# Token tiles turned by DMA transposes instead of TensorE's, in an attention and two-expert-layer kernel

## The chip, the cores and the metric

The kernel runs on one core of a Trainium2 chip. The metric is the device time of one execution in microseconds (us); lower is better. The profile comes from one execution. In it PE is TensorE (PEld its weight loads), DVE is VectorE, ACT is ScalarE, POOL is GpSimd and SP is SyncE, whose queue issues all of this kernel's DMAs.

## What is computed

Inputs are 4 sequences of 576 tokens with 8 heads of 64. An attention with a memory term gives 512 numbers per token; two gated expert layers of 512 to 1536 to 512 follow.

```python
scores = scale * q @ k.T                      # causal
local = softmax(scores) @ v
q_p = where(q > 0, q, exp(q) - 1) + 1
mem_out = (q_p @ M_prev) / (q_p @ z_prev + 1e-6)
x = g * mem_out + (1 - g) * local             # g = sigmoid(beta); 2304 x 512
xn = x / sqrt(mean(x * x) + 1e-6) * rms_g     # first layer's norm
y = (silu(xn @ w_gate) * (xn @ w_val)) @ w_out
out = (sigmoid(y @ w_gate2) * (y @ w_val2)) @ w_out2
```

## The kernel before, in words

The 2304 tokens go in five groups. Group -1 holds the first 128 tokens of each sequence (512 tokens); its attention is written out by hand at the start. Groups 0 to 3 hold the other 448 tokens of one sequence each. The main loop (from line 976) takes a group through both expert layers, l = 0 and 1, each in NF = 12 slices of 128 hidden units: `hidden` makes the two products `pg` and `pv` of a slice (12 matmuls each, in `mm3`, line 782), `out_share` (line 831) adds the slice's 12 matmuls to the four output tiles `po`. While group g is in these layers, the attention of group g + 1 is done in 36 steps, listed by `att_steps` (line 905) and handed out at a fixed rate as the slices go by, all of them four slices ahead of the end (six in group -1). The last five steps are the norm (`att_norm`) and four times `next_xT`, one for each 128-token tile.

Matmuls contract over partitions, so the expert layers need a group's tokens with the 512 channels on partitions. The attention leaves them with tokens on partitions, in the tile `x`. `att_xT` (line 602) turns them: VectorE writes the normalized tile `xn` (line 605), TensorE transposes its four 128x128 blocks in float32 into a PSUM tile `pxt` (line 610), ScalarE copies that as float16 into the high half of the token tile `ha` (line 614), and VectorE writes the rest, PSUM minus high half, as float16 into the low half (line 615). A product then is three float16 matmuls per block of channels: high by high, high by low, low by high. The fourth tile overlaps the third by 64 tokens; only its last 64 are kept. `half_tokens` (line 900) makes the token tile of shape 128 x 2 x 4 x 512.

Tile pools: `ap_` (line 76) has one buffer for each name unless the call says otherwise; `xn` has two; `psa`, the PSUM pool of `pxt` and of the attention's products, has two. A new tile in a buffer waits until all that use the old one are through. The tile `x` has one buffer: the next sequence's values are loaded into it by `att_v` (lines 137 and 138) when the last `xn` has been written.

Weights come from device memory. Group -1 makes float32 and group 0 float16 parts of them once and stores these; later loads (lines 753 and 756) go into 13 slots in turn, on SP's queue, some slices ahead of their use. The same queue holds the loads of q and k (line 182), the stores of outputs (lines 889 and 894) and of weight parts (line 688).

The order of the instructions on each engine is not that of the text: the framework's planner goes through the program with durations that it assumes, and puts on each engine the ready instruction that comes first in the text. The hardware then runs each engine's list in that order.

Of the kernel before, what the change touches and what calls it, by code (L numbers as in the profile page):

```python
# [9 lines left out]
F32 = mybir.dt.float32  # L10
F32R = mybir.dt.float32r
F16 = mybir.dt.float16
# [4 lines left out]
ALU = mybir.AluOpType  # L17
# [39 lines left out]
def attn_moe_moe_kernel(ctx, tc, qT, kT, qk0, v, mz, beta, w8, rms_g, outT):  # L57
# [6 lines left out]
    nc = tc.nc  # L64
    B, H, D, S = qT.shape
    NP = H // 2
    DM = H * D
    KD = DM // 128
# [7 lines left out]
    ap_ = ctx.enter_context(tc.tile_pool(name="ap", bufs=1))  # L76
# [7 lines left out]
    ident = const.tile([128, 128], F32, name="ident")  # L84
# [4 lines left out]
        out=tri, in_=tri, compare_op=ALU.is_ge, fill=NEG, base=0, pattern=[[1, 128]], channel_multiplier=-1  # L89
# [35 lines left out]
    for i in range(2):  # L125
        t = const.tile([128, S], F32R, name=f"q2_{i}")
# [6 lines left out]
    st = {}  # L133
# [468 lines left out]
    def att_xT(g, t, xt):  # L602
        s = st[g]
        xn = ap_.tile([128, DM], F32, tag="xn", bufs=2, name="xn")
        nc.vector.scalar_tensor_tensor(
            out=xn, in0=s["x"][:, t, :], scalar=s["ri"][:, t:t + 1], in1=g_bc, op0=ALU.mult, op1=ALU.mult
        )
        ps = late["ps"].tile([128, KD, 128], F32, tag="pa", name="pxt")
        for k in range(KD):
            nc.tensor.transpose(ps[:, k, :], xn[:, k * 128:(k + 1) * 128], ident)  # L610
        o = 64 if t == 3 else 0
        c0 = 128 * t
        n = 128 - o
        nc.scalar.copy(out=xt[0][:, :, c0:c0 + n], in_=ps[:, :, o:128])
        nc.vector.tensor_tensor(
            out=xt[1][:, :, c0:c0 + n], in0=ps[:, :, o:128], in1=xt[0][:, :, c0:c0 + n], op=ALU.subtract
        )


    late, first_raw = {}, []  # L620
    ring = {"w": 0, "top": 0, "raw": 0}
# [76 lines left out]
    for i in range(2):  # L698
        t = const.tile([128, 512], I32, name=f"top{i}")
# [196 lines left out]
    def wide_tokens(tags):  # L896

        return [xp.tile([128, KD, NMAX], F32R, tag=t, name="x" + t) for t in tags]

    def half_tokens(tag):  # L900

        t = xp.tile([128, 2, KD, NMAX], F16, tag=tag, name="h" + tag)
        return [t[:, 0], t[:, 1]]

    def att_steps(g):
        yield lambda: att_v(g)

        for h in range(H + 1):
            if h < H:
                yield lambda h=h: att_qk(g, h)  # L910
                yield lambda h=h: att_scores(g, h)

            if h == 0:
                yield lambda: att_vmax(g)
            if h == 1:
                yield lambda: att_vsplit(g)
            if h > 0:
                yield lambda h=h: att_av(g, h - 1)
                if h % 2 == 0:
                    yield lambda h=h: att_mem(g, h // 2 - 1)  # L920
        yield lambda: att_norm(g, 0, 4)
        for t in range(4):
            yield lambda t=t: next_xT(g, t)

    def att_first():


        att_load0()
        xt = wide_tokens("ab")
        ws, hs = [[], []], [htiles(-1, 0, f) for f in range(2)]  # L930
        do = first_stages(xt)
        do.update(slice_stages(xt, ws, hs))
        traced, before = nc.cur_bb.bb.instructions, {}
        for name in ORDER.split():
            n = len(traced)
            if name.startswith("fill"):
                do["fill"](int(name[4:]))
            else:
                do[name]()
            for i in traced[n:]:  # L940
                if i.engine in before:
                    tc.add_manual_dep(
                        i,
                        before[i.engine].name,
                        mybir.DependencyInfo(mybir.DependencyClass.NoSync, mybir.DependencyReason.DATA),
                        reason="order",
                    )
                before[i.engine] = i
            if name == "Cb3":
                z["hi"] = before[mybir.EngineType.Activation]  # L950
            if name == "Vb3":
                z["lo"] = before[mybir.EngineType.DVE]

        ring["raw"] = 0
        return xt, ws, hs

    def next_xT(g, t):
        if t == 0:
            st["xt"] = half_tokens("a")
        att_xT(g, t, st["xt"])  # L960

    xt, early_ws, early_hs = att_first()
    zctx.close()
# [11 lines left out]
    for g in range(-1, B):  # L975
        n = 512 if g < 0 else S - 128
# [6 lines left out]
        for l in range(2):  # L983
# [5 lines left out]
            for f in range(NF + 1):  # L989
                if f < NF:  # L990
                    if f >= early:
                        if g > 0 and l == 1 and f == NWIDE:
                            mid = NF if g < B - 1 else NF // 2 + 2
                            for e, c in ((nc.vector, slice(NWIDE, mid)), (nc.gpsimd, slice(mid, NF))):
                                if c.start < c.stop:
                                    e.tensor_scalar(
                                        out=unit[2][:, c],
                                        in0=unit[1][:, c],
# [25 lines left out]
            xn = wide_tokens("cd") if l == 0 else None  # L1024
            for d in range(KD):
                evacuate(l, d, n, g, po[d], xn)
            if l == 0 and g >= 0:
                xh = half_tokens("b")
                halve_tokens(n, po, xh)
            if l == 0 and g < 0:  # L1030
                token_scale()
            xt = xn
        xt = st.pop("xt", None)
# [55 lines left out]
```

## Time and profile before

| | |
|---|---|
| median of 3 runs | 1075.39 us (1075.17 to 1077.75) |
| the profiled execution | 1077.86 us, with a span of 1076.1 us |
| TensorE busy | 97% of the span |
| VectorE, ScalarE busy | 69%, 51% |
| mean granted TensorE clock | 0.991 of full speed |
| DMA, mean | 203 GB/s |

Busy time is the time in which an engine runs an instruction; for TensorE the ends of pipelined matmuls are modelled, so overlapping matmuls of 0.35 us each may follow each other every 0.19 us. The chain of waits is followed back from the last instruction, at each step to what released it. "Issue to landing" of a DMA runs from its issue on SP to the moment when its completion is seen.

### The profile page before, as it was taken

Reading aid. Unit: us, or ns where it says so; the run is one execution under the profiler, and the core shown is the slowest. Engines: PE = TensorE matmul, PEld = TensorE weight load, DVE = VectorE, ACT = ScalarE, POOL = GpSimd, SP = SyncE. Lnnn points to the kernel's source line nnn. Section 1 sums busy time; section 2 is a strip of 40 time slices with the busy share of each in tenths; the row PEclk is TensorE's granted clock in tenths of the full one; section 3 lists DMA queues with packets and bytes.
Section 4 is the critical chain, followed back from the end, with each engine's and each line's share of the span. In section 5 each row is a group of like instructions: output and inputs, shape, how many; then the busy total and the mean of one; then the engine's idle time right before and its main releaser. Section 6 shows DMA issues by size and latency. Waiting matters only on the chain.

```text
span 1076.1 us, 17841 instructions
## 1 busy us (share of the span) xinstructions
PE 1043.3 (97%) x6505; PEld 756.1 (70%) x6509; DVE 738.0 (69%) x1588; ACT 551.1 (51%) x1074; POOL 93.1 (9%) x85
## 2 busy tenths in 40 slices
PE   7899999999899999998999999999999999999998
PEld 5778887888666677665677876766777766667665
DVE  5969999998788788885747876485687653224211
ACT  4768877776587658763434553353346332112111
POOL 2301012000011011100101010000010100000000
PEclk8999999999999999999999999999999999999999
DMA  6499998985567855875547445555554445454440
GB/s 263 149 361 375 323 351 269 329 274 169 191 225 263 284 177 152 283 237 198 166 136 218 149 155 171 183 182 159 186 171 132 132 138 174 146 184 157 142 133 34
DMA packets 90679, 218.49 MB, mean 203 GB/s; under 512 B 10720, under 2 KB 16864, under 8 KB 90464
## 3 DMA queue, kind: packets, MB, share of 16 engines
q1 hardware_dynamic: 90592, 217.36, 61.5%
q8 instruction: 51, 0.84, 0.3%
q14 instruction: 36, 0.29, 0.1%
HBM read 173.28 MB, written 44.04 MB: 202 GB/s over the span
## 4 chain that ended last, share of the span: by engine, by line
PE 71%; DVE 12%; DMA 9%; ACT 4%; issue 3%; SPq 1%; POOL 0%; ACTq 0%; DVEq 0%; POOLq 0%
PE pg L786 21%; PE po L839 21%; PE pv L786 20%; PE ps L206 3%; DMA w<-kept 2%; DMA x<-in_v 1%; DMA rawl<-in_w 1%; DMA g_bc<-in_rms_g 1%; PE pm L566 1%; DMA qd<-in_qT 1%; PE pav L517 1%; PE pav L519 1%; PE pav L518 1%; DVE vl L170 1%; ACT sc L197 1%
## 5 line engine op out<-in xcount | busy, mean ns | idle before, releaser
L803 ACT ACTIVATE t<-pg,unit 128x448 f32<-128x448 f32 x88 | 55.5, 630 | 148.2 <-PE pg L786 148.0
L839 PE MATMUL po<-h,ws 128*128 128x448 f32 (+1 forms) x504 | 121.1, 384 | 0.0
L839 PEld LDWEIGHTS po<-h,ws 128*128 128x128 f32 x504 | 93.3, 188 | 11.9
L501 POOL PARTITION_ALL_REDUCE mb<-mx x32 | 60.2, 1881 | 466.0 <-DVE mx L497 448.7
L786 PEld LDWEIGHTS <-wr 128*128 128x128 f16 x648 | 60.2, 98 | 56.8 <-issue 6.1
L786 PEld LDWEIGHTS <-ws 128*128 128x128 f16 x624 | 58.2, 98 | 54.8 <-issue 5.5
L813 DVE SCALAR_TENSOR_TENSOR t<-t,pv 128x448 f32<-128x448 f32 (+1 forms) x60 | 37.9, 632 | 84.0 <-PE pv L786 83.3
L839 PE MATMUL po<-h,wl 128*128 128x448 f32 (+1 forms) x384 | 93.8, 386 | 0.2 <-DVE h L823 0.2
L839 PE MATMUL po<-h,wr 128*128 128x448 f32 x360 | 83.7, 377 | 0.7 <-DVE h L819 0.7
L786 PEld LDWEIGHTS <-wl 128*128 128x128 f16 x504 | 47.8, 99 | 50.0 <-issue 9.4
L805 DVE SCALAR_TENSOR_TENSOR t<-t,pg 128x448 f32<-128x448 f32 (+2 forms) x60 | 37.2, 620 | 64.4 <-ACT t L803 64.3
L839 PEld LDWEIGHTS po<-h,wl 128*128 128x128 f32 x384 | 71.1, 188 | 9.9 <-DVE h L823 0.6
L473 ACT COPY sc<-ps 128x64 f32<-128x64 f32 (+3 forms) x128 | 47.0, 371 | 57.4 <-DVE sc L468 29.8
L839 PEld LDWEIGHTS po<-h,wr 128*128 128x128 f32 x360 | 67.1, 188 | 8.0 <-DVE h L819 1.1
L818 ACT CAST h<-t 128x448 fp32r<-128x448 f32 (+1 forms) x70 | 40.5, 579 | 55.9 <-DVE t L807 50.5
L206 PE MATMUL ps<-qq,kk 128*128 128x448 f32 (+2 forms) x160 | 57.2, 363 | 7.3 <-ACT sc L473 6.3
L200 DVE TENSOR_TENSOR pt<-sc,pt 128x1536 f16<-128x1536 f32 x32 | 56.1, 1752 | 10.0 <-ACT pt L199 9.8
L197 ACT ACTIVATE sc<-sc 128x1536 f32<-128x1536 f32 x32 | 47.5, 1483 | 22.7 <-DVE sc L510 22.5
L819 DVE TENSOR_TENSOR h<-t,h 128x448 fp32r<-128x448 f32 (+1 forms) x70 | 45.2, 646 | 19.3 <-ACT h L818 18.6
L822 ACT ACTIVATE h<-t,unit 128x448 fp32r<-128x448 f32 x40 | 26.7, 668 | 53.5 <-DVE t L813 53.2
L786 PEld LDWEIGHTS <-wrl 128*128 128x128 f16 x336 | 31.4, 98 | 30.6 <-issue 3.2
L199 ACT CAST pt<-sc 128x1536 f16<-128x1536 f32 x32 | 46.8, 1463 | 4.7 <-PE pav L519 4.6
(245 smaller groups left out, 2484.5 us busy)
## 6 DMA issues: line engine op xcount, KB each, us to landing
raw<-in_w SPq DMA_DIRECT2D x50, 511.8 KB, 6.4
ws<-parts SPq DMA_DIRECT2D x34, 512.0 KB, 3.5
wr<-parts SPq DMA_DIRECT2D x32, 512.0 KB, 3.5
w<-kept SPq DMA_DIRECT2D x50, 256.0 KB, 4.4
kept<-w SPq DMA_DIRECT2D x48, 256.0 KB, 5.4
wl<-parts SPq DMA_DIRECT2D x24, 512.0 KB, 3.5
rawl<-in_w SPq DMA_DIRECT2D x22, 511.8 KB, 6.5
ws<-half SPq DMA_DIRECT2D x41, 256.0 KB, 2.7
```

The lines of the kernel that those rows point to most:

```text
L197: nc.scalar.activation(out=sc[:, 0:n], in_=sc[:, 0:n], func=AF.Exp, scale=scale)
L199: nc.scalar.copy(out=pt[:, 0, 0:n], in_=sc[:, 0:n])
L200: nc.vector.tensor_tensor(out=pt[:, 1, 0:n], in0=sc[:, 0:n], in1=pt[:, 0, 0:n], op=ALU.subtract)
L206: nc.tensor.matmul(ps[:, c0:c0 + n], kk[:, k0:k0 + 128], r[:, q0:q0 + n], start=(i == 0), stop=(i == 1 and not mask))
L473: nc.scalar.copy(out=sc[:, d:d + n], in_=ps[:, c:c + n])
L501: nc.gpsimd.partition_all_reduce(mb[:, 0:448], mx[:, 0:448], channels=128, reduce_op=bass_isa.ReduceOp.max)
L786: nc.tensor.matmul(ps[:, 0:n], w[:, a, k * 128:(k + 1) * 128], x[b][:, k, o:o + n], start=(i == 0), stop=(i == 3 * KD - 1))
L803: nc.scalar.activation(out=t, in_=pg[:, 0:n], func=AF.Tanh, scale=u[:, 0:1] if half else 0.5)
L813: nc.vector.scalar_tensor_tensor(out=t, in0=t, scalar=1.0, in1=pv[:, 0:n], op0=ALU.add, op1=ALU.mult)
L818: nc.scalar.copy(out=hi, in_=t)
L819: nc.vector.tensor_tensor(out=lo, in0=t, in1=hi.bitcast(F32), op=ALU.subtract)
L839: nc.tensor.matmul(po[d][:, 0:n], w[2][:, a, c], hh[:, b, 0:n], start=(f == 0 and i == 0), stop=(f == NF - 1 and i == 2))
```

## The change

In groups 0 to 3 the normalized tile is split into its two float16 halves while its tokens are still on partitions, into a new tile `xs` of 128 x 2 x 512 (from the pool with one buffer for each name). One DMA transpose per 128-token tile, issued by SP, then moves both halves, eight blocks of 128x128, into the token tile, all channels on partitions. The PSUM tile and TensorE's four transposes per tile go. For the fourth tile only the last 64 tokens (partitions 64 to 127 of `xs`) are transposed; its split takes all 128. `half_tokens` also returns the whole tile, so that one DMA can write both halves.

```diff
         nc.vector.scalar_tensor_tensor(
             out=xn, in0=s["x"][:, t, :], scalar=s["ri"][:, t:t + 1], in1=g_bc, op0=ALU.mult, op1=ALU.mult
         )
-        ps = late["ps"].tile([128, KD, 128], F32, tag="pa", name="pxt")
-        for k in range(KD):
-            nc.tensor.transpose(ps[:, k, :], xn[:, k * 128:(k + 1) * 128], ident)
+        xs = ap_.tile([128, 2, DM], F16, tag="xs", name="xs")
+        nc.scalar.copy(out=xs[:, 0], in_=xn)
+        nc.vector.tensor_tensor(out=xs[:, 1], in0=xn, in1=xs[:, 0], op=ALU.subtract)
         o = 64 if t == 3 else 0
         c0 = 128 * t
-        n = 128 - o
-        nc.scalar.copy(out=xt[0][:, :, c0:c0 + n], in_=ps[:, :, o:128])
-        nc.vector.tensor_tensor(
-            out=xt[1][:, :, c0:c0 + n], in0=ps[:, :, o:128], in1=xt[0][:, :, c0:c0 + n], op=ALU.subtract
+        nc.sync.dma_start_transpose(
+            out=xt.rearrange("p a k n -> p (a k) n")[:, :, c0:c0 + 128 - o], in_=xs[o:128].rearrange("p a d -> p (a d)")
         )
...
     def half_tokens(tag):
 
         t = xp.tile([128, 2, KD, NMAX], F16, tag=tag, name="h" + tag)
-        return [t[:, 0], t[:, 1]]
+        return [t[:, 0], t[:, 1], t]
...
     def next_xT(g, t):
         if t == 0:
             st["xt"] = half_tokens("a")
-        att_xT(g, t, st["xt"])
+        att_xT(g, t, st["xt"][2])
```

## Rows read from the trace of the kernel before

**Rows 1.** Page, part 1: busy us (share of the span) x instructions of each engine

```profile
PE 1043.3 (97%) x6505; PEld 756.1 (70%) x6509; DVE 738.0 (69%) x1588; ACT 551.1 (51%) x1074; POOL 93.1 (9%) x85
```

**Rows 2.** Page, part 4: the chain that ended last, shares of the span by engine

```profile
PE 71%; DVE 12%; DMA 9%; ACT 4%; issue 3%; SPq 1%; POOL 0%; ACTq 0%; DVEq 0%; POOLq 0%
```

**Rows 3.** Busy us by stretch: us; PE, PEld, DVE, ACT, POOL; PEclk, DMA share, GB/s

```profile
474.00:506.00 32.00, 28.49 (x146) 19.77 (x147) 19.17 (x52) 10.01 (x22) 0.67 (x1) 0.95 0.55 185
680.00:710.00 30.00, 28.80 (x154) 19.20 (x153) 19.07 (x46) 12.38 (x24) 0.66 (x1) 1.00 0.59 191
...
506.00:680.00 174.00, 171.60 (x1191) 122.47 (x1190) 121.59 (x259) 77.03 (x126) 14.14 (x9) 1.00 0.54 166
...
290.00:294.00 4.00, 1.34 (x4) 0.70 (x5) 3.87 (x8) 1.02 (x2) 0.00 (x0) 0.81 1.09 389
```

**Rows 4.** Instructions on tile `pxt`: ns min/median/max, first and last start us, forms

```profile
L610 PE MATMUL pxt<-ident,xn x64: 270/272/273, 281.4 to 893.5; 128*128 128x128 f32 x64
L614 ACT CAST ha<-pxt x16: 356/585/592, 282.0 to 893.8; 128x512 f16<-128x512 f32 x12, 128x256 f16<-128x256 f32 x4
L615 DVE TENSOR_TENSOR ha<-pxt,ha x16: 414/680/692, 283.9 to 894.6; 128x512 f16<-128x512 f32 x12, 128x256 f16<-128x256 f32 x4
```

**Rows 5.** The chain that ended last, pieces near 520 and 890 us: start, us, what

```profile
516.48 0.81 PE ps L206 x4
...
886.53 0.87 PE pxt L610 x8
...
898.28 2.41 PE po L839 x12
```

**Rows 6.** Groups by line and form, weight splits: busy us, mean ns of one

```profile
L682 ACT ACTIVATE wr<-w,s 128x512 f16<-128x512 f32 x16 | 10.8, 715 | 0.8 <-DVE s L651 0.7
...
L683 DVE SCALAR_TENSOR_TENSOR wr<-w,s,wr 128x512 f16<-128x512 f32 x16 | 11.5, 743 | 1.0 <-ACT wr L682 1.0
```

**Rows 7.** Timeline of SP near 470 us: start us, us, what was issued

```profile
470.17 0.40 SPq L753 DMA_DIRECT2D wrl<-half  x1
```

**Rows 8.** Timeline at B0: start us, us, engine, line [idle before, releaser]

```profile
275.59 1.42 DVE L605 SCALAR_TENSOR_TENSOR xn<-x,ri,g_bc 128x512 f32<-128x512 f32 x2
...
293.58 3.38 PE L786 MATMUL pg<-ha,wl 128*128 128x448 f16 x11
```

**Rows 9.** Timeline at B1, the same columns

```profile
482.73 1.42 DVE L605 SCALAR_TENSOR_TENSOR xn<-x,ri,g_bc 128x512 f32<-128x512 f32 x2
...
487.33 0.68 DVE L823 SCALAR_TENSOR_TENSOR h<-t,unit,h 128x448 fp32r<-128x448 f32 x1 [0.74 <-ACT h L822]
...
488.35 1.42 DVE L605 SCALAR_TENSOR_TENSOR xn<-x,ri,g_bc 128x512 f32<-128x512 f32 x2 [0.33 <-PE pxt L610]
...
493.39 0.74 PE L839 MATMUL po<-h,wr 128*128 128x448 f32 x2
...
500.36 3.12 PE L839 MATMUL po<-h,wrl 128*128 128x448 f32 x8 [2.14 <-DVE h L823]
...
504.03 2.28 PE L786 MATMUL pg<-ha,wrl 128*128 128x448 f16 x11
```

**Rows 10.** Timeline at B2, the same columns

```profile
685.65 1.41 DVE L605 SCALAR_TENSOR_TENSOR xn<-x,ri,g_bc 128x512 f32<-128x512 f32 x2
...
705.75 2.25 PE L786 MATMUL pg<-ha,wl 128*128 128x448 f16 x11
```

**Rows 11.** Timeline at B3, the same columns

```profile
881.25 1.42 DVE L605 SCALAR_TENSOR_TENSOR xn<-x,ri,g_bc 128x512 f32<-128x512 f32 x2
...
900.52 2.44 PE L786 MATMUL pg<-ha,ws 128*128 128x448 f16 x12
```

**Rows 12.** DMA: KB each, median us to landing; and line 753's 132 loads of 256 KB

```profile
out_T<-o SPq DMA_DIRECT2D x4, 256.0 KB, 5.0
...
DMA to landing us min/median/max: 2.4/2.7/6.4
```

## The prediction

> **What bounds the kernel now.** I read the page's totals first [rows 1]: TensorE is busy for 97% of the span, VectorE for 69%, ScalarE for 51%. The chain of waits that ended last says the same [rows 2]: 71% of it is TensorE. The busy time of chosen stretches [rows 3] then splits the span: inside a group TensorE is busy 171.60 of 174.00 us, but in the 32 us around the change from the first group of 448 to the second only 28.49. So TensorE work taken away inside a group is time gained; at a change of groups what counts is when the next group's tokens are ready, because its first products need all four token tiles. The edit sits just there, at four changes that I call B0 (from the 512 first tokens to group 0) to B3 (group 2 to 3).
>
> **What it removes.** 64 transposes of 128x128. One lasts 272 ns [rows 4], but they are pipelined: in the chain eight take 0.87 us [rows 5]. Eight such bundles are 8 x 0.87 = 7.0 us, 1.74 at each change. The 16 copies (ScalarE, 585 ns, the four half ones 356) and 16 subtractions (VectorE, 680 and 414) out of PSUM go too [rows 4].
>
> **What it adds.** The same 16 copies and 16 subtractions, now from the whole 128x512 tile in SBUF. The nearest rows of that shape are the weight splits [rows 6]: 715 ns on ScalarE, 743 on VectorE. In all that is 16 x 0.715 = 11.4 us against 8.4, and 11.9 against 9.8: 3 and 2 us more, on engines that are free for a third of the span or more while TensorE works. As work I cost them at nothing; as delay they count, below. And SP issues 16 DMA transposes. A plain issue held SP for 0.40 us [rows 7], some 6 us in all on a queue that mostly waits.
>
> **What it moves: a new chain.** Before, each normalized tile `xn` went through TensorE, a copy and a subtraction, with two PSUM tiles to overlap neighbours. After, the tile `xs` comes from a pool with one buffer. So the copy of tile t+1 may not write until the transfer of tile t has ended, and a group's four tiles form one chain: copy, subtraction, transfer, copy, subtraction, transfer, and so on. A step costs 0.715 + 0.743 = 1.46 us of work. Both engines are mostly within some other instruction of 0.6 to 0.7 us, so I add 0.27 us of waiting to each and call a step 2.0. With L for one transfer from issue to landing, the last tile lands 0.75 (xn) + 4 x 2.0 + 4L = 8.8 + 4L after the first xn starts.
>
> How long may that be? The first xn starts at 275.59, 482.73, 685.65 and 881.25 us, and the bulk of the next group's first product at 293.58, 504.03, 705.75 and 900.52 [rows 8 to 11]: 18.0, 21.3, 20.1 and 19.3 us. At B0 to B2 that is the launch with eleven matmuls; one goes out ahead of it. TensorE can also bring work forward while it waits: at B3 the old group's last output share, 2.4 us; at B0 to B2 about eight score products of the next group's first head, 1.6 us (four take 0.81) [rows 5]. No change of group can win more than its 1.74 us.
>
> **The unknown, L.** No transposing DMA is in the trace. Bounds from landings [rows 12]: plain loads of 256 KB landed in 2.4 us at the least, 2.7 in the middle, 6.4 at the most. The nearest row is the store of 256 KB in pieces of 512 bytes (line 889), 5.0 us. A transfer of whole rows would be nearer the 2.7; a transpose writes pieces of 256 bytes, which speaks for the 5.0, but that store ran while the DMA engines were full (share 1.09 near B0, 0.55 and 0.59 at B1 and B2 [rows 3]), which speaks for less. I take the middle of 2.7 and 5.0, 3.9 us. Then the last tile lands after 8.8 + 15.6 = 24.4 us, and the losses are 24.4 - 18.0 - 1.6 = 4.8, then 1.5 and 2.7 in the same way, and 24.4 - 19.3 - 2.4 = 2.7: 11.7 us. The 1.74 us are inside these: TensorE has that work no longer, ahead of a moment that has become later.
>
> The clock adds something. At B1 TensorE idled 2.14 us in one piece [rows 9], and the granted clock then fell to the lower level for a while (0.95 in that stretch), as at B0 (0.81), where the eleven products took 3.38 us instead of the 2.28 of B1 [rows 3, 8, 9]: 1.1 us lost. At B2 it stayed full [rows 3]. With idle times of 4 us at B2 and B3 I expect two more such falls, 2.2 us. The sum is **+13.9 us**.
>
> The Trainium skill (Advanced Engine Details and Errata, section X-Bar Transpose (TRN2)) speaks for a lower L: it holds transposing DMAs on trn2 to be as fast as regular ones. No row here shows one; by it the sum would be that of the first rival.
>
> Queues behind the waits. ScalarE now waits for a transfer ahead of three of a group's copies, and the tanh and the h split of the running product stand behind it. VectorE finishes a low half of h at 488.01 and TensorE uses it from 493.39 [rows 9]: a hold of up to 5 us is covered, beyond it each hold costs its excess. On SP a transpose waits for its subtraction, with weight loads behind it. They run ahead: the load issued at 470.17 feeds the eleven products at 504.03 [rows 7, 9], some 30 us later, and four steps of 5.9 us are 24. That cover is thin; without it the next group's weights are late, one load of 2.7 us at a time. The load of the next `x` (line 137) must follow the last xn, which now waits for the second subtraction: it ends 0.75 + 2.0 + 3.9 + 2.0 + 0.75 = 9.4 us after the first one starts, instead of 7.0 [rows 9]. The scores' scaling hangs on `x`; a microsecond each at B1 and B2 is left to the range.
>
> **How it stands to the runs.** The profiled execution took 1077.86 us, 1.8 of it around a span of 1076.1; the median of the runs shown is 1075.39. I add the sum to the median: 1075.4 + 13.9 = 1089. About 0.3% (3.2 us) is what a measurement of this kernel can tell from no change.
>
> **Rivals.**
> 1. *The transfer is as quick as a plain load and is hidden* (faster). With L = 2.7 the last tile lands after 19.6 us: B0 comes out at 0, the others win their whole 1.74, so -5.2 us, 1070. With 2.4 it is -6.4, 1069. For it: the DMA engines are half idle at B1 and B2, and both ends of the transfer lie in SBUF. Against it: the short pieces, and line 889. It decides below L = 3.2, where the sum is zero.
> 2. *The transfer goes block by block* (much slower). If its eight 128x128 blocks follow each other rather than spread over the DMA engines, L reaches the 6.4 us of the slowest load; the last tile lands after 34.4 us, the losses are 14.8 + 11.5 + 12.7 + 12.7 = 52 us, 1127. Nothing in the trace shows it; plain transfers do spread. The Trainium skill (VectorE: DVE Perf Modes, section The three transpose paths) gives 1309 ns for one such block by DMA, against 390 on TensorE; eight in a row would be an estimated 10.5 us, and the time about 1190. No run here shows that either.
> 3. *The tiles are late, but the planner finds cover* (no change). It lays each engine's order out anew and may put score products and output shares into the wait. It needs some 14 us more of them than the 7 I count; VectorE gates the scores, so little else is ready.
>
> That the change does not do what it says can hardly be: the transposes leave the program text.
>
> **How the numbers follow.** My forecast, L from 3.3 to 5.6: 0.45. Rival 1: 0.31. Rival 2, with anything over 5.6: 0.11. Rival 3: 0.13. Faster is rival 1 and a little of rival 3 (0.33), no change most of rival 3 (0.11), slower the forecast and rival 2 (0.56). The forecast's own range is 1079 to 1116: L = 3.3 gives 2.4 - 0.9 + 0.3 + 0.3 = 2.1 and one fall of the clock, 1.1; L = 5.6 gives 11.6 + 8.3 + 9.5 + 9.5 + 2.2 = 41. The range that should hold 8 in 10 takes in rival 1, from 1067, and ends at 1113; rival 2 stays out.
>
> **What would show it.** In the profile after: no line 610; 16 transposes on SP whose time to landing is L, the number that decides; copies into `xs` with idle time ahead of them that a DMA ended, about L each for three tiles of four; TensorE's first product of a group waiting some 4 us, and for a DMA; more stretches at the lower clock. If L is under 3.2 and TensorE does not wait for the transfers, I am wrong and rival 1 is right; if the copies do not wait for transfers at all, my chain is wrong whatever L is.

## The result, and the profile after

The changed kernel takes 1085.65 us (median of 4; 1083.79 to 1088.24) against 1076.57 (median of 4) for the kernel before, timed beside it: a ratio of 1.0084, 95% interval 1.0055 to 1.0113. It is slower by 9 us. The profiled execution has a span of 1083.6 us, 7.5 more than before.

In the totals (part 1 of the page) TensorE is busy 6.0 us less than in [rows 1] and idle 13.5 us more. VectorE and ScalarE are busy 2.8 and 3.8 us more; 2 and 3 were costed.

```profile
PE 1037.3 (96%) x6441; PEld 749.5 (69%) x6445; DVE 740.8 (68%) x1588; ACT 554.9 (51%) x1074; POOL 90.5 (8%) x85
```

The instructions on the tile `xs` stand in place of [rows 4]: each line gives ns min/median/max and the first and last start. The lines under "sat idle" give us and times, by what ended the idle time.

```profile
L609 ACT CAST xs<-xn x16: 602/619/620, 275.5 to 905.0; 128x512 f16<-128x512 f32 x16
L610 DVE TENSOR_TENSOR xs<-xn,xs x16: 681/692/695, 276.2 to 905.7; 128x512 f16<-128x512 f32 x16
L613 SPq DMA_TRANSPOSE ha<-xs x16: 1200/1240/1607, 276.9 to 906.4; - x16
its engine sat idle before it (us, times) until:
  DMA ha<-xs: 23.8, 10
  ACT xs L609: 14.6, 6
...
DMA to landing us min/median/max: 2.5/3.1/6.8
```

The unknown of the prediction, L, is 3.1 us in the middle, and each issue holds SP for 1.24 us. ScalarE sat 23.8 us in ten idle stretches until a transfer had ended: the chain through the one buffer is there. TensorE's waits, longest in total first (us, times, longest):

```profile
PE ps L206 <- ACT sc L473: 12.3, 7, 4.9
PE pg L783 <- DMA ha<-xs: 9.7, 3, 6.8
PE pav L517 <- ACT pt L199: 3.4, 2, 1.8
```

TensorE now waits 9.7 us for the token tile, 6.8 of them at B0. Its waits for ScalarE's score copies (`sc`) doubled; in the kernel before they were:

```profile
PE ps L206 <- ACT sc L473: 6.3, 4, 2.7
```

At B0 such waits (4.9 and 1.9 us) come ahead of the wait for the tile, so TensorE idles there for longer than 6.8 us. Timeline of B0, the answer to [rows 8]; the copy of the third tile starts at 286.19, its transfer at 291.23:

```profile
274.74 1.42 DVE L605 SCALAR_TENSOR_TENSOR xn<-x,ri,g_bc 128x512 f32<-128x512 f32 x2
...
276.89 6.07 SPq L613 DMA_TRANSPOSE ha<-xs  x2
...
283.14 0.45 SPq L137 DMA_DIRECT2D x<-in_v  x1
...
286.19 0.60 ACT L609 CAST xs<-xn 128x512 f16<-128x512 f32 x1
...
288.46 0.69 DVE L610 TENSOR_TENSOR xs<-xn,xs 128x512 f16<-128x512 f32 x1
...
291.23 1.61 SPq L613 DMA_TRANSPOSE ha<-xs  x1
...
296.97 0.62 ACT L609 CAST xs<-xn 128x512 f16<-128x512 f32 x1 [2.20 <-DMA ha<-xs]
...
299.52 1.42 SPq L613 DMA_TRANSPOSE ha<-xs  x1
...
305.54 3.83 PE L783 MATMUL pg<-ha,wl 128*128 128x448 f16 x12 [6.83 <-DMA ha<-xs]
```

From the first xn to the first product: 30.8 us, where [rows 8] had 18.0. The third tile shows how a step grows. The second transfer landed at 284.4, but ScalarE is in the weight splits of group 0, and the third tile's copy starts 1.8 us later. That copy (0.60) ends at 286.79, but VectorE is in the same weight splits and subtracts at 288.46; that is done at 289.15, but SP stands in its own order behind stores of weight parts and issues at 291.23; the transfer lands 5.7 us later, while loads and stores of weights keep the DMA engines full. The load of the next `x` (1.25 MB, issued at 283.14) was no longer beside it: it had landed by 290.6. In the busy time by stretch, the columns of [rows 3]:

```profile
286.00:290.00 4.00, 1.89 (x9) 0.95 (x7) 3.32 (x8) 3.77 (x9) 0.00 (x0) 1.00 0.99 332
290.00:294.00 4.00, 0.00 (x0) 0.00 (x0) 3.97 (x7) 1.35 (x3) 0.00 (x0) 0.67 1.09 384
294.00:298.00 4.00, 1.30 (x5) 1.06 (x5) 3.97 (x12) 1.80 (x6) 0.37 (x1) 0.50 1.13 291
298.00:302.00 4.00, 0.71 (x2) 0.61 (x3) 3.40 (x13) 2.77 (x10) 1.94 (x2) 0.50 1.07 311
302.00:306.00 4.00, 0.47 (x2) 0.24 (x2) 3.90 (x8) 4.00 (x9) 0.00 (x0) 0.50 1.15 265
```

TensorE works 4.4 us of these 20, and the granted clock falls to the lower level for some 17 us (in the next 4 us it is still 0.70).

The tile is what TensorE waited for last ahead of B0's bulk. But the chain that ended last in this profile does not run over a transfer of group 0. From 283 to 313 us it runs over the load of `x`, then over VectorE's and ScalarE's work on the next group's attention, and comes back to TensorE where that waits for the softmax weights `pt`:

```profile
283.14 6.67 DMA x<-in_v
...
296.10 4.99 DMA kd<-in_kT
...
306.51 2.73 DVE vl L170 x4
...
311.02 1.77 DVE pt L200
```

```profile
312.84 0.20 PE L519 MATMUL pav<-vh,pt 128*128 128x65 f16 x1 [0.66 <-DVE pt L200]
```

So a second path, over VectorE, is about as long as that of the tile. With the instructions in this order, by this chain, a tile that came earlier would have left TensorE waiting for `pt`.

The other changes of group (answers to [rows 9 to 11]):

```profile
492.14 1.42 DVE L605 SCALAR_TENSOR_TENSOR xn<-x,ri,g_bc 128x512 f32<-128x512 f32 x2
...
516.48 4.16 PE L783 MATMUL pg<-ha,wrl 128*128 128x448 f16 x12 [2.62 <-DMA ha<-xs]
```

```profile
689.88 1.41 DVE L605 SCALAR_TENSOR_TENSOR xn<-x,ri,g_bc 128x512 f32<-128x512 f32 x2
...
712.89 2.43 PE L783 MATMUL pg<-ha,wl 128*128 128x448 f16 x12 [0.70 <-ACT vh L169]
```

```profile
889.70 1.42 DVE L605 SCALAR_TENSOR_TENSOR xn<-x,ri,g_bc 128x512 f32<-128x512 f32 x2
...
909.01 2.43 PE L783 MATMUL pg<-ha,ws 128*128 128x448 f16 x12 [0.27 <-DMA ha<-xs]
```

From these rows and [rows 8 to 11] the time splits at the bulk of each group's first product:

| stretch | before | after | difference |
|---|---|---|---|
| start to B0 | 293.58 | 305.54 | +12.0 |
| B0 to B1 | 210.45 | 210.94 | +0.5 |
| B1 to B2 | 201.72 | 196.41 | -5.3 |
| B2 to B3 | 194.77 | 196.12 | +1.3 |
| B3 to the end | 175.58 | 174.59 | -1.0 |

The loss lies ahead of B0; from there on the changed kernel is the faster by 4.5 us. B1 comes 24.3 us after its first xn (21.3 before), yet costs little: the planner put 20 score products there (there were two between first xn and bulk before), and 12 are missing, to its gain, in the stretch behind. At B0 there are 19, where there were four.

### The profile page after: what moved, and what is told of

It reads as the page before. It is cut to its first block, busy times and chain, and to the rows that moved or that the text cites. A ratio compares the mean times of both kernels' runs of the same rounds, so it can differ in the third digit from the quotient of the medians.

```text
span 1083.6 us, 17761 instructions
## 1 busy us (share of the span) xinstructions
PE 1037.3 (96%) x6441; PEld 749.5 (69%) x6445; DVE 740.8 (68%) x1588; ACT 554.9 (51%) x1074; POOL 90.5 (8%) x85
## 2 busy tenths in 40 slices
DMA packets 105527, 222.16 MB, mean 205 GB/s; under 512 B 25568, under 2 KB 31712, under 8 KB 105312
## 4 chain that ended last, share of the span: by engine, by line
PE 74%; DMA 8%; DVE 6%; ACT 4%; issue 2%; SPq 0%; POOL 0%; ACTq 0%; DVEq 0%
PE po L836 22%; PE pg L783 22%; PE pv L783 21%; PE ps L206 3%; DMA ha<-xs 2%; DMA x<-in_v 1%; PE pm L566 1%; DMA out_T<-o 1%; PE pav L517 1%; PE pav L519 1%; DMA kd<-in_kT 1%; PE pav L518 1%; DMA ph<-in_qT 1%; ACT sc L197 1%; DMA w<-kept 1%
## 5 line engine op out<-in xcount | busy, mean ns | idle before, releaser
L200 DVE TENSOR_TENSOR pt<-sc,pt 128x1536 f16<-128x1536 f32 x32 | 56.2, 1756 | 11.0 <-ACT pt L199 10.6
L517 PE MATMUL pav<-vh,pt 128*128 128x65 f16 x448 | 47.2, 195 | 3.4 <-ACT pt L199 3.4
```

The source lines that it names most:

```text
L200: nc.vector.tensor_tensor(out=pt[:, 1, 0:n], in0=sc[:, 0:n], in1=pt[:, 0, 0:n], op=ALU.subtract)
L517: nc.tensor.matmul(ps, ph, vh1[:, vt, h, :], start=first, stop=False)
```

## The experiments

Theory A: the loss is the chain through the one buffer of `xs`, which makes the last tile late. B: the transfers as such (SP's hold, disturbed DMA queues). C: the planner's new order. Ratios are to the kernel before, timed on the same chip; its median moved between 1076.6 and 1079.6 us over these comparisons, so the ratio counts.

| run | us | ratio | 95% interval |
|---|---|---|---|
| the change | 1085.65 | 1.0084 | 1.0055 to 1.0113 |
| four buffers | 1068.67 | 0.9903 | 0.9885 to 0.9922 |
| two buffers | 1064.51 | 0.9864 | 0.9843 to 0.9885 |
| not turned | 1066.67 | 0.9879 | 0.9856 to 0.9902 |
| both ways at once | 1088.63 | 1.0089 | 1.0069 to 1.0108 |
| DMA in group 0 alone | 1086.26 | 1.0074 | 1.0058 to 1.0090 |
| DMA in groups 1 to 3 alone | 1075.61 | 0.9971 | 0.9956 to 0.9986 |
| load of x behind | 1089.41 | 1.0107 | 1.0090 to 1.0124 |
| ScalarE's queue | 1093.56 | 1.0151 | 1.0129 to 1.0172 |
| two buffers in group 0 alone | 1072.35 | 0.9952 | 0.9933 to 0.9971 |
| two buffers, elsewhere | 1066.69 | 0.9900 | 0.9875 to 0.9925 |

**Four buffers.** SBUF has no room for more `xs` tiles at the kernel's start, so three of a group's four tiles lie in a tile of the softmax weights, which is free then.

```diff
-        xs = ap_.tile([128, 2, DM], F16, tag="xs", name="xs")
+        if t == 0:
+            s["xs"] = ap_.tile([128, 3, 2, DM], F16, tag="pt", name="xs3")
+        xs = s["xs"][:, t] if t < 3 else ap_.tile([128, 2, DM], F16, tag="xs", name="xs")
```

> The change with a buffer for each of a group's four split tiles: three lie in the attention's weight tile, which is idle at that time, the fourth in the old one. Theory A (the one buffer chains copy, subtraction and transfer, and the late last tile is the loss): no copy waits for a transfer, the last tile lands some 12 to 14 us after the first xn instead of 23 to 31, TensorE no longer waits for the token tile (9.7 us now), and the time is 1069 to 1074 us, below the kernel before by about the 7 us of transposes. Theory B (the transfers themselves cost: SP held 1.2 us by each, DMA engines and queues disturbed): waits move elsewhere and the time stays at 1082 to 1087 us. Theory C (the planner's new order is what costs): any time, with the waits of TensorE for the token tile gone and others of the same sum in their place.

1068.67 us, 11 us under the kernel before and just below the range of theory A. In the instructions on `xs`, no idle time of ScalarE or VectorE ends with a transfer any more:

```profile
L615 SPq DMA_TRANSPOSE ha<-xs x16: 1222/1328/2411, 277.5 to 883.7; - x16
its engine sat idle before it (us, times) until:
  DVE xn L605: 9.8, 6
  ACT xs L611: 1.0, 2
...
DMA to landing us min/median/max: 3.1/4.0/8.2
```

L is longer here, 4.0 us, with transfers that now overlap, and the kernel is still 1.8% faster than the change (0.9903 against 1.0084). So the number that the prediction hung everything on was not the one that decides; four L in a row were. "TensorE no longer waits" was not met in full: 3.7 us remain, 2.4 of them at B0.

**Two buffers.**

```diff
-        xs = ap_.tile([128, 2, DM], F16, tag="xs", name="xs")
+        xs = ap_.tile([128, 2, DM], F16, tag=("xs", "pt")[t % 2], name="xs")
```

> The change with two buffers for the split tiles instead of one. Theory A: a copy waits for the transfer two tiles back, so the last tile lands about 14 to 16 us after the first xn, still inside the 18 to 21 us that the kernel before had: 1069 to 1076 us. Theory B: 1082 to 1087 us, as with one.

1064.51 us, the fastest of all runs, better than expected. At B0 the bulk starts 13.8 us after the first xn:

```profile
275.42 1.42 DVE L605 SCALAR_TENSOR_TENSOR xn<-x,ri,g_bc 128x512 f32<-128x512 f32 x2
...
289.17 2.43 PE L783 MATMUL pg<-ha,wl 128*128 128x448 f16 x12 [1.95 <-DMA ha<-xs]
```

**Not turned.** The edit in `att_xT`, in place of the new lines:

```diff
+        src = xn.rearrange("p (k n) -> p k n", n=128)[:, :, o:128]
+        nc.scalar.copy(out=xt[:, 0, :, c0:c0 + n], in_=src)
+        nc.vector.tensor_tensor(out=xt[:, 1, :, c0:c0 + n], in0=src, in1=xt[:, 0, :, c0:c0 + n], op=ALU.subtract)
```

> Leaves the turning out: each normalized tile of groups 0 to 3 is split straight into the token tile, with its tokens still on partitions; no transposes on TensorE, no DMA transposes, the same copies and subtractions. It gives what the removed transposes are worth alone. By the sum of the prediction 7.0 us, so 1068 to 1071 us; if the last tile's earlier arrival also fills the idle time that the kernel before has at the first two changes of group (2 to 4 us), down to 1064.

1066.67 us, a gain of 1.2% or 13 us (interval 10.6 to 15.5): more than the 7.0 of the sum, while the 9 to 11 us with the idle time added lie partly inside the interval. In the profiles the gain lies in two stretches, 6.0 us ahead of B0's bulk and 6.8 between those of B1 and B2. Two buffers do as well with 16 DMA transposes in them, so with two buffers the transfers cost nothing that can be seen: theory B falls.

**Both ways at once.** Beside the kernel before, each tile is also split into four buffers and turned by a DMA transpose into a spare tile:

```diff
+        xs = s["xs"][:, t] if t < 3 else ap_.tile([128, 2, DM], F16, tag="mx", name="xs")
+        nc.scalar.copy(out=xs[:, 0], in_=xn)
+        nc.vector.tensor_tensor(out=xs[:, 1], in0=xn, in1=xs[:, 0], op=ALU.subtract)
+        spare = ap_.tile([128, 8, 128], F16, tag=("spare", "mb")[t % 2], name="spare")
+        nc.sync.dma_start_transpose(out=spare[:, :, 0:n], in_=xs[o:128].rearrange("p a d -> p (a d)"))
```

> The kernel before, with all that the change adds put beside it and nobody waiting for it: each normalized tile is also copied and subtracted into a split tile (four buffers) and turned by a DMA transpose into a spare tile that nothing reads. Theory A: work and transfers are hidden, 1074 to 1079 us, as the kernel before. Theory B: the transfers' hold on SP and on the DMA engines shows, 1084 us or more. Theory C: a shift of some us either way without a wait that belongs to the transfers.

1088.63 us: theory A's range is missed, and it is the figure of B, but no wait of TensorE is for a transfer. The longest group is for the old subtraction from PSUM:

```profile
PE ps L206 <- DVE ha L615: 9.3, 3, 4.0
```

VectorE and ScalarE do the split twice here, and the PSUM tile that the scores want stays held until the subtraction from PSUM is through. The run mixes added work with added transfers and does not decide between A and B; the three before it do. It points to VectorE's time at the changes of group as a cost, but VectorE is busy 9.8 us more here, and in the change only 2.8, which the prediction costed at nothing as work.

**DMA in one part of the groups.** Group 0 by DMA with one buffer, groups 1 to 3 by TensorE, and the reverse; the edit puts the old lines back under a condition, `if not (g == 0):` in the first, `if not (g > 0):` in the second.

> The change at one place: only group 0's tokens are turned by DMA (one buffer), groups 1 to 3 by TensorE as before. If the loss is made at the first change of group, where the chain took 31 us and the profile of the change has its longest wait (6.8 us, bulk of the first product 12 us later than before): 1083 to 1090 us. If each change of group loses its share: 1078 to 1080.

> The rest of the change: groups 1 to 3 by DMA with one buffer, group 0 by TensorE. If the loss is made at the first change of group, the other three cost nothing and keep their 5 us of transposes: 1070 to 1076 us, faster than the kernel before. If each loses its share: 1081 to 1084.

1086.26 and 1075.61 us: the change in group 0 alone loses what the whole change loses, the change in the other three gains 0.3% (interval 0.1 to 0.4%). In the first the wait at B0 is the same as in the change, to 0.01 us:

```profile
306.66 4.64 PE L795 MATMUL pg<-ha,wl 128*128 128x448 f16 x12 [6.84 <-DMA ha<-xs]
```

Two things keep these runs from splitting the loss cleanly. They do not add up: +0.74% and -0.29% make 0.45% where the change has 0.84%, which the intervals just allow. And in the profile with group 0 alone B0's bulk comes 13.1 us later than before, the end 8.6: 4.5 us are won back behind B0 though no later transpose is gone. The 4.5 us of the table above, then, need not be a gain of the other three changes of group.

**The load of x behind the last transfer.** The load of the next group's values is kept behind the fourth transfer on SP's queue:

```diff
+        st["turn"] = next(i for i in reversed(nc.cur_bb.bb.instructions) if i.engine == mybir.EngineType.SP)
...
+        with ExitStack() as behind:
+            if "turn" in st:
+                behind.enter_context(tc.issue_after(st["turn"]))
```

> The change with one buffer, and the load of the next group's values x (1.25 MB) put behind the last transfer on SP's queue. In the profile of the change the transfers that follow that load land after 5.4 to 6.8 us, the others after 2.5 to 3.7. If that contention is a real part of the late last tile, the chain gets 3 to 6 us shorter at the first three changes of group, TensorE's wait for the token tile falls from 9.7 to 5 us or less, and the time to 1077 to 1083 us; the values come later, which may give 1 to 3 us of it back. If only the buffer counts, 1084 to 1088.

The chain did get shorter: transfers land after 2.9 us in the middle and 5.4 at most (6.8 before), and at B0 the bulk starts 27.3 us after the first xn instead of 30.8; at B1 and B2 it comes 5.9 and 4.5 us sooner. But TensorE's wait for the token tile is 11.0 us in all, and the time is 1089.41 us, a miss. The load of the values is now issued at 297.63 instead of 283.14. VectorE stands 2.9 us before it, its other work behind that, and the `t` that TensorE needs comes at 315.38, so TensorE gets a second wait right behind the first:

```profile
301.10 3.71 PE L787 MATMUL pg<-ha,wl 128*128 128x448 f16 x12 [7.84 <-DMA ha<-xs]
...
306.21 2.47 DVE L149 TENSOR_REDUCE am<-x 128x1 f32<-128x512 f32 x4 [2.91 <-DMA x<-in_v]
...
315.38 0.61 DVE L806 SCALAR_TENSOR_TENSOR t<-t,pg 128x448 f32<-128x448 f32 x1
...
316.04 4.64 PE L787 MATMUL pg<-ha,wr 128*128 128x448 f16 x12 [8.96 <-DVE t L806]
```

So with the load out of the way the chain at B0 is 3.5 us shorter, 3.2 of them in the landings of its last two transfers (3.9 and 4.6 us instead of 5.7 and 6.0), and the load's place in the queue is worth more than that. This fits the chain shown above, which ran over this load and not over the tile.

**ScalarE's queue.** `nc.scalar.dma_start_transpose` in place of `nc.sync`.

> The change with one buffer, its transfers issued by ScalarE's queue instead of SP's. In the profile of the change two of the four transfers of the first change of group were ready 2.1 and 1.2 us before SP came to them. If SP's order is a real part, the chain there gets 3 us shorter and the time falls to 1080 to 1084 us; ScalarE is then held 1.2 us by each issue, 20 us in all on an engine that is half idle. If it is no part: 1084 to 1090.

1093.56 us, a miss. With SP no longer in the way B0's bulk is at 32.1 us after the first xn instead of 30.8. The wait only changed its place: the third tile's subtraction comes 4.6 us after its copy, ScalarE issues the transfer 1.0 us after that, and each issue holds it for 1.2 us.

```profile
285.73 0.61 ACT L609 CAST xs<-xn 128x512 f16<-128x512 f32 x1
...
290.95 0.68 DVE L610 TENSOR_TENSOR xs<-xn,xs 128x512 f16<-128x512 f32 x1
...
292.64 1.30 ACTq L613 DMA_TRANSPOSE ha<-xs  x1
...
300.23 0.62 ACT L609 CAST xs<-xn 128x512 f16<-128x512 f32 x1 [3.08 <-DMA ha<-xs]
```

**Two buffers in group 0 alone.**

```diff
+        xs = ap_.tile([128, 2, DM], F16, tag=("xs", "pt")[t % 2 if g == 0 else 0], name="xs")
```

> The change with two buffers for group 0's tiles alone, one for groups 1 to 3. If the one buffer at the first change of group is the whole loss: the last tile of group 0 lands some 13 us after the first xn there instead of 31, TensorE's longest wait for the token tile is under 3 us, and the time is 1068 to 1076 us, below the kernel before. If what the other changes of group lose counts too: 1080 or more.

1072.35 us: a second buffer at one of four places turns the change from 0.8% slower into 0.5% faster. B0's bulk is 14.5 us after the first xn, with a wait of 2.7 us:

```profile
273.28 1.41 DVE L605 SCALAR_TENSOR_TENSOR xn<-x,ri,g_bc 128x512 f32<-128x512 f32 x2
...
287.74 2.43 PE L783 MATMUL pg<-ha,wl 128*128 128x448 f16 x12 [2.66 <-DMA ha<-xs]
```

**Two buffers, elsewhere.** The second buffer lies in the tile of row maxima: `tag=("xs", "mx")[t % 2]`.

> Two buffers everywhere, as in the run with two, but the second one lies in the attention's tile of row maxima instead of in that of the softmax weights. Nothing in the chain differs. If two buffers as such give the 1064.5 us: within 2 us of it. If that figure hangs on the order in which the planner happens to put the next group's attention (four buffers gave 1068.7 with the tile of softmax weights held longer): 1066 to 1072.

1066.69 us, ratio 0.9900 against 0.9864; the intervals overlap (0.9875 to 0.9885). It lies just past the first case's bound and inside the second's: a choice that leaves the chain alone moves the time by 2 us, by the ratios 0.4%, no more than the intervals allow for. That much of any single figure here may be theory C, and it may be why four buffers came out 4 us behind two; that was not settled.

These runs also tell what the one buffer costs at B1 to B3. With the second buffer in group 0 alone the ratio is 0.9952, with it everywhere 0.9900 and 0.9864, so that the one buffer at the other three changes of group costs 0.5 to 0.9%, 5 to 10 us. Against the kernel before this does not show, since the change's gains there cover it.

No run separates the buffer from the order that the planner lays out for it. In the four runs with two or four buffers in group 0 the load of `x` is issued 5.4 us after the first xn, in the change 8.4; since the chain at B0 ran over this load, part of what the second buffer gives may come that way and not through the tile. The runs show that the second buffer removes the loss, not by which of the two paths.

## Why the prediction was right, and where not

The direction held, and so did the main mechanism: the one buffer chains copy, subtraction and transfer, and it costs more than 64 transposes are worth; a second buffer turns the loss into a gain. That the late last tile is all of it was not shown: at B0 a path over the load of `x` and VectorE is as long. Forecast +13.9 us, measured +9.1, inside the range. The last tile landed 30.8, 24.1, 22.9 and 19.2 us after the first xn at B0 to B3, by the starts and landings of the fourth transfers; the mean, 24.2, stands beside the 24.4 of the prediction, but the spread is not in it. That the sum came out near is in part luck: too little at B0, too much at the other three. By the prediction's own steps:

- *What it removes*, 7.0 us: too low. The run without any turning gains 13 us, so the cap of 1.74 us for a change of group was wrong too. How much of the rest is idle time at the changes of group and how much the planner's order was not separated.
- *L = 3.9 us*: too long where the DMA engines are free (2.5 to 3.7 us), too short where they are not. At B0 the four transfers landed after 2.9, 2.7, 5.7 and 6.0 us, at B1 after 3.3, 2.7, 5.4 and 2.6, the third behind the load of `x`. The mean over all 16 is 3.7 us, the middle 3.1. The prediction let L decide, with the turn at 3.2: with 3.1 its own sum comes to -1.1 us, with 3.7 to +8.5, the clock not counted. So the single number could not settle it; the slow landings and the waits of B0 did. The rule of the Trainium skill (Advanced Engine Details and Errata, section X-Bar Transpose (TRN2)) came nearer than the store of line 889: the middle of 3.1 us stands beside 2.6 for a plain 256 KB load in the same profile. The block-by-block time of the second rival did not show: eight whole blocks landed together in 2.7 us at the least (the 2.5 is a fourth tile, of half the size).
- *A step of 2.0 us beside L*: this term failed at B0, and it is where the sum over the four places went wrong. There the third tile waited 1.8 us for ScalarE, 1.7 for VectorE and 2.1 for SP, and took 5.7 to land; I had charged 0.54 us for all waiting, as for engines in the middle of another instruction, not for queues that stand in order behind other work. Without L and the first xn a step took 3.2 us at B0, and 2.3, 1.6 and 1.6 at B1 to B3. B0's bulk came 12.0 us later, where I had 4.8.
- *Losses of 1.5, 2.7 and 2.7 us at B1 to B3*: against the kernel before these did not come. The groups by DMA with one buffer in 1 to 3 alone are 3 us faster than before; what the one buffer costs there, 5 to 10 us against two, is covered. At B3 the chain took 19.3 us, as TensorE did before, with L near 3. At B1 TensorE waited, but over work that it had brought forward: rival 3's cover, which I had put at eight products and which was 20 (19 at B0).
- *The clock*: no fall at B2 and B3, since TensorE did not idle there, but falls of some 17 and 10 us at B0 and B1. The first product's twelve matmuls took 3.83 and 4.16 us instead of 2.43, 3.1 us in all, against the 1.1 that the kernel before lost at B0.
- *The hold on ScalarE*, costed at nothing under 5 us: right. It was idle for 23.8 us ahead of the copies, and TensorE's waits for h are under 2 us in all.
- *SP's cover of 30 us for weight loads*: it held; no wait of TensorE in the profile after is for a weight load. The hold by an issue, 1.24 us and not 0.40, matters in the chain alone.

## What to carry to other kernels

Moving work to a DMA turned 0.4 us of an engine's time per tile into a latency of about 3 us. With one buffer four tiles pay that, and every wait of the queues around it, four times in a row; with two it was nearly hidden here. Look at the place where the queues are fullest, not only at the average one: against the kernel before, the loss came from one of four changes of group, the one at which ScalarE, VectorE, SP and the DMA engines were all busy with other work. The one buffer cost something at the other three too, hidden under what the change saved there, and only the run with two buffers everywhere brought it out. A tile that is idle at that time can lend the missing buffer when SBUF is full, and that turned a change that lost 0.8% into one that gains 1.4%.

## What the runs showed of the hardware

A DMA transpose of 128 x 1024 float16 from SBUF to SBUF lands in 2.7 to 3.7 us when nothing large is in flight (one of 64 x 1024 in 2.5 to 2.6), but its issue holds the issuing queue for 1.20 to 1.61 us, on SP as on ScalarE (1.21 to 1.35), and for up to 2.46 in the run with two buffers, where a plain weight load of line 753 (L750 in the profile after) holds SP for 0.32 in most rows. Its data goes in small packets: the count of those under 512 bytes rose from 10,720 to 25,568 while 3.67 MB more were moved, about 250 bytes for each, and the bytes read from and written to HBM did not change.

```profile
DMA packets 105527, 222.16 MB, mean 205 GB/s; under 512 B 25568, under 2 KB 31712, under 8 KB 105312
...
HBM read 173.28 MB, written 44.04 MB: 201 GB/s over the span
```

With the 1.25 MB load of `x` still in flight the same transfer took 5.4 us at B1 and 6.8 at B2 to land; at B0, with that load landed but the DMA engines full (share 1.07 to 1.15), two took 5.7 and 6.0.
